# Evicting the P-times-V bank in two halves, by VectorE and by a pinned ScalarE copy

## The chip, the cores and the metric

The kernel runs on one core of a Trainium2 chip. The metric is device time in microseconds of one execution, the median over several; a profile of one execution stands beside it. The engines are called PE (TensorE matmul), PEld (TensorE weight load), DVE (VectorE), ACT (ScalarE), POOL (GpSimd) and SP (SyncE, which starts transfers).

## The reference

A block with two branches over x of 2048 rows and 640 columns, mixed by a gate per row. Branch a is attention with 32 heads of 20 columns in 4 segments of 512 rows, plus a memory of the segments before; branch b is a gated feed-forward layer of 1728 columns. In float32:

```python
for s in range(4):                                   # segments of 512 rows
    logits = einsum("bhqd,bhkd->bhqk", qs, ks) * scale + causal_mask
    a_dot = einsum("bhqk,bhkd->bhqd", softmax(logits), vs)
    pq = phi(qs)                                     # t + 1 where t > 0, else exp(t)
    a_mem = einsum(pq, M) / (einsum(pq, z) + 1e-6)
    o = g * a_mem + (1 - g) * a_dot                  # g = sigmoid(beta) per head
    M, z = M + phi(ks)^T vs, z + sum(phi(ks))
a = o @ wo
b = (silu(x @ w1) * (x @ w3)) @ w2
return sigmoid((x * gate_w).sum(-1)) * a + (1 - ...) * b
```

## The kernel before

All weights and activations are split into a high and a low part (fp32r), and each projection is three passes over five blocks of 128 input columns: 15 matmuls of 512 columns into one PSUM bank. PE's queue is in the order in which the program is written (`manual_schedule` for PE alone). The other engines' queues are ordered by the framework's scheduler, from a simulated timeline. `here` (L102, `keep_in_program_order`) pins one instruction behind the one that was traced just before it on the same engine; unpinned instructions may pass each other.

The eight PSUM banks are handed out by `bank_tile` (L111) in turn from a list. A bank that a projection holds while it is being filled goes back to the end of the list when it is full (`filled`, L122).

Attention works on quads of four heads, 32 quads in all, one for every 40 slots of the outer loop. The work of a quad `m` is placed in two visits inside the stream of projections, a big one at slot 5 and a small one at slot 17 (`VISITS`, L758). A big visit begins when no projection holds a bank. It issues, on PE, in this order:

- s0 of quad m: queries by keys, to find the row maxima (`s_fill`, L594; DVE reduces each region, L609, "junk")
- t0 and t1 of quad m-1: keys by queries with the maximum already subtracted (`t_fill`, L625; ACT takes the exponential into the tile P, L641; POOL masks the diagonal blocks, L645)
- o of quad m-2: P times V for four heads into one bank (`pv_quad`, L650)
- t3 of quad m-1, s2 of quad m, t2 of quad m-1, s1 of quad m

Each s and t fill takes two banks, o takes one. The big visits of quads 0 and 1 lack o, and that of quad 1 is cut in two; the last two big visits have no s. After the visit the stream of projections goes on: g and u (up, L253; ACT's tanh L514, DVE's products L515 and L521, ACT's rounding of the high part L106), f (down, L555; DVE adds, L563), q and k (L253; ACT rounds L280, exponentials L283 and L284; DVE L285 and L287), v (L381), op (output projection, L805), nd (memory read).

The instruction in question is L659: DVE copies o's bank (128 partitions by 512 columns) to the tile `oq`, and SP stores that to memory (L661).

Of the kernel before, what the change touches and what calls it, by code (L numbers as in the profile page):

```python
# [11 lines left out]
AF = mybir.ActivationFunctionType  # L12
# [5 lines left out]
P = 128  # L18
# [6 lines left out]
SCALE = DH ** -0.5  # L25
BIG = -1.0e38
# [12 lines left out]
def gated_mix(ctx: ExitStack, tc: tile.TileContext, xT, wqk, wv, w13, w2, w2h, wo, beta, out):  # L39
    nc = tc.nc  # L40
# [61 lines left out]
    here = tc.keep_in_program_order  # L102
    last = {}
# [7 lines left out]
    def bank_tile(name, hold=None):  # L111


        k = free.pop(0)
        ps = pp.tile([P, L], F32, tag=f"b{k}", name=name, bufs=1)
        if hold:
            held[k] = -hold
        else:
            free.append(k)
        return ps  # L120
# [348 lines left out]
    def job_q(cs, mb, alloc={}):  # L469
        i = w_add(wqk[mb], D)  # L470
        return [(3.5, q_block(c, mb, i, alloc.get(c))) for c in cs]

    def job_q2(cs, mb, alloc={}):

        i = w_add(wqk[mb], D)
        j = w_add(wqk[mb + 1], D)
        return [(3.5, q_block(c, m, k, alloc.get(c), j if c == cs[-1] and m > mb else i))
                for c in cs for m, k in ((mb, i), (mb + 1, j))]
# [89 lines left out]
    oall, heads, pairs = {}, {}, {}  # L568

    def load_pair(p):  # L570

        j = 2 * p
        c, h = divmod(j, H)
        t = qk[p // 2 % 2][:, :, p % 2]
        for mb in {DH * h // P, (DH * h + 2 * DH - 1) // P}:
            assert ("q", c, mb) in stored and ("k", c, mb) in stored
        assert ("v", c, 3) in stored
        for i in range(2):
            here(nc.gpsimd.dma_start(t[64 * i:64 * i + RH], qkd[c][RH * (h + i):RH * (h + i + 1)]))  # L579
        if h % 8 == 0:  # L580
            bank["v"] = v = vg[j // 8 % NVG]
            here(nc.sync.dma_start(v[:, :, :VG], vd[c][:, :, VE * h:VE * h + VG]))
        if p % 2 == 0:
            bank["m"] = sp.tile([P, 16], F32, tag="m", name=f"m{j}", bufs=2)
        for i in range(2):
            o = VE * (h % 8 + i)
            heads[j + i] = dict(c=c, h=h + i, v=bank["v"][:, :, o:o + 32])
        pairs[p] = dict(t=t, m=bank["m"])
# [5 lines left out]
    def s_fill(m, f):  # L594

        todo = S_FILL[f]
        ps = [bank_tile(f"s{m}_{f}_{i}") for i in range(2)]
        for n, (k, qb, o) in enumerate(todo):
            w = P * (qb + 1)
            for i in range(2):  # L600
                q, key = (pairs[2 * m + k]["t"][64 * i:64 * i + RH, x] for x in range(2))
                nc.tensor.matmul(ps[i][:, o:o + w], q[:, qb * P:(qb + 1) * P], key[:, :w],  # L602
                                 start=n == 0, stop=n == len(todo) - 1, skip_group_check=True)
        for i in range(2):
            for k, qb, o in todo:
                w = P * (qb + 1)
                junk = sp.tile([P, L], BF, tag="junk", name="junk", bufs=1)
                a = 8 * i + 4 * k + qb
                nc.vector.tensor_tensor_reduce(out=junk[:, :w], in0=ps[i][:, o:o + w], in1=mask[:, L - w:],  # L609
                                               scale=1.0, scalar=-3.0e38, op0=ALU.add, op1=ALU.max,  # L610
                                               accum_out=pairs[2 * m]["m"][:, a:a + 1])
# [10 lines left out]
            dst = qk[p // 2 % 2][RH + a:RH + a + 65:64, 0].rearrange("h k (b n) -> h (k b) n", n=P).bitcast(F32)  # L622
            after(4, lambda d=dst, r=16 * a: here(nc.scalar.dma_start(d, mr[r:r + 16])))

    def t_fill(m, f):  # L625

        todo = T_FILL[f]
        ps = [bank_tile(f"t{m}_{f}_{i}") for i in range(2)]
        for n, (k, kb, o) in enumerate(todo):
            u = pairs[2 * m + k]  # L630
            if "P" not in u:
                u["P"] = sp.tile([P, 2, 1280], F32, tag="P32", name=f"P{2 * m + k}", bufs=NP)
            for i in range(2):
                q, key = (u["t"][64 * i:64 * i + RH + 2, w] for w in range(2))
                nc.tensor.matmul(ps[i][:, o:o + L - kb * P], key[:, kb * P:(kb + 1) * P], q[:, kb * P:],  # L635
                                 start=n == 0, stop=n == len(todo) - 1, skip_group_check=True)

        outs = [(k, PSEG[kb][0], o, L if (kb, len(todo)) == (1, 2) else L - kb * P) for k, kb, o in todo if kb != 3]
        for i in range(2):
            for k, o, b, n in outs:  # L640
                last["exp"] = nc.scalar.activation(pairs[2 * m + k]["P"][:, i, o:o + n], ps[i][:, b:b + n],  # L641
                                                   AF.Exp, scale=SCALE)
        for k, o, n in (((0, 0, 1),), ((0, 512, 1),), ((0, 896, 2),), ((1, 0, 1),), ((1, 512, 1), (1, 896, 2)))[f]:
            d = pairs[2 * m + k]["P"][:, :, o:o + n * P].rearrange("p h (a b) -> p h a b", b=P)
            nc.gpsimd.affine_select(d, d, pattern=[[0, 2], [0, n], [1, P]], base=0, channel_multiplier=-1,  # L645
                                    compare_op=ALU.is_ge, fill=0.0)
# [3 lines left out]
    def pv_quad(p):  # L650

        ps = bank_tile(f"o{p}")
        for kb, (o, n) in enumerate(PSEG):
            for i in range(4):
                nc.tensor.matmul(ps[32 * i:32 * i + 32, kb * P:], heads[2 * p + i]["v"][:, kb],  # L655
                                 pairs[p + i // 2]["P"][:, i % 2, o:o + n],
                                 start=kb == 0, stop=kb == 3, skip_group_check=True)
        ot = sp.tile([P, L], F32, tag="oq", name=f"oq{p}", bufs=1)
        nc.vector.tensor_copy(ot, ps)  # L659
        c, h = heads[2 * p]["c"], heads[2 * p]["h"]  # L660
        nc.sync.dma_start(od[c][h:h + 4].rearrange("h e n -> (h e) n"), ot)  # L661
        q = p // 2 % 8
        for b in OUT.get(q, ()):
            after(8, o_load, c, b)
        if q == 7:
            after(6 if c < NSEG - 1 else 2, o_sums, c)
# [77 lines left out]
    def after(n, f, *a):  # L744
        soon.append([n, f, a])

    def tick():
        for e in list(soon):
            e[0] -= 1
            if e[0] <= 0:  # L750
                soon.remove(e)
                e[1](*e[2])
# [4 lines left out]
    BIG, SMALL = 5, 17  # L757
# [3 lines left out]
    def attention():  # L761

        for m in range(-1, NQUAD + 2):
            for n in range(40):
                if m == -1 and n < 40 - LEAD:
                    continue

                todo = VISITS.get(n, ()) if m != 1 else {BIG: VISITS[BIG][:3], BIG + 6: VISITS[BIG][4:]}.get(n, VISITS.get(n, ()))
                todo = [(kind, m - q, f) for kind, q, *f in todo if 0 <= m - q < NQUAD]
                if todo:  # L770
                    yield "amid" if len(todo) < 4 else "between"
                    for kind, q, f in todo:
                        if kind == "o":
                            pv_quad(2 * q)
                        else:
                            (s_fill if kind == "s" else t_fill)(q, *f)
                    if n == SMALL and 0 <= m < NQUAD:
                        after(4, max_rows, 2 * m)
                elif n in ((24, 36) if m < 0 else (BIG + 7, SMALL + 1)) and m + 1 < NQUAD:
                    load_pair(2 * (m + 1) + (n > BIG + 7 if m >= 0 else n > 24))  # L780
                tick()
                yield m
# [118 lines left out]
    q = job_q(B[:1], 0, {2: big_tile})  # L901
# [5 lines left out]
    q = job_q2(B, 3)  # L907
# [21 lines left out]
    for n, (_, g) in enumerate(head):  # L929
# [7 lines left out]
        elif n == 7:  # L937
            gates()
    stores(True)
    att = attention()  # L940

    def begin():
# [102 lines left out]
```

## Time and profile before

| what | value |
|---|---|
| median of 3 runs | 1108.1 us (1107.41 to 1110.36) |
| the profiled execution | 1108.07 us |
| its span, first to last instruction | 1106.4 us |
| PE busy | 1095.1 us, 99% |
| DVE busy | 593.5 us, 54% |
| ACT busy | 381.2 us, 34% |
| POOL busy | 583.3 us, 53% |
| granted TensorE clock | 1.00 |

In the profile's rows, "out<-in" names the tile written and the tiles read; "xcount" is how many instructions a row merges; a time in brackets is how long the engine had been idle and which instruction released it. Matmuls are pipelined and their ends are modelled, so two matmuls' durations overlap, and PE's busy share is no measure of how well it is used. In the timeline the columns are the start and the length of the stretch in us.

### The profile page before, as it was taken

What the parts mean: (1) busy time and instruction counts of PE and PEld (TensorE: products, weight loads), DVE (VectorE), ACT (ScalarE), POOL (GpSimd) and SP (SyncE); (2) the same over time, 40 slices, a digit from 0 to 9 for tenths busy, and PEclk for the clock granted to TensorE, in tenths of its full rate; (3) what the DMA queues carried; (4) which work ended last, traced back from release to release, by engine and by line L of the source; (5) the groups of instructions that cost most, each with busy time, mean ns of one, the idle gap of its engine ahead of it and who ended that gap; (6) DMA issues with size and microseconds to landing.
All of it is one profiled execution on the core that took longest, in us unless ns stands there. A gap on an engine that the chain in (4) does not pass through costs nothing.

```text
span 1106.4 us, 17867 instructions
## 1 busy us (share of the span) xinstructions
PE 1095.1 (99%) x6285; PEld 854.0 (77%) x6285; DVE 593.5 (54%) x1708; ACT 381.2 (34%) x826; POOL 583.3 (53%) x729
## 2 busy tenths in 40 slices
PE   9999999999999999999999999999999999999997
PEld 7988877777777777787977777777777777777786
DVE  5032564355555554366154678875557665551645
ACT  6244233343233122145244543424333332233120
POOL 5055556366366363565175547556764555565253
PEclk9999999999999999999999999999999999999999
DMA  8266943335165132535268967455654443432122
GB/s 314 102 212 220 281 117 82 95 82 127 47 164 125 57 78 94 156 98 191 96 202 271 287 204 193 103 157 138 166 139 111 103 104 90 117 105 86 52 79 95
DMA packets 87545, 153.20 MB, mean 138 GB/s; under 512 B 11584, under 2 KB 25184, under 8 KB 87456
## 3 DMA queue, kind: packets, MB, share of 16 engines
q1 hardware_dynamic: 63040, 106.30, 30.5%
q0 software_dynamic: 20384, 38.68, 15.6%
q10 hardware_dynamic: 4032, 7.08, 1.8%
q8 instruction: 50, 0.82, 0.3%
q14 instruction: 39, 0.32, 0.1%
HBM read 96.56 MB, written 54.54 MB: 137 GB/s over the span
## 4 chain that ended last, share of the span: by engine, by line
PE 94%; DVE 3%; ACT 1%; DMA 1%; issue 1%; ACTq 0%; SPq 0%; DVEq 0%
PE g L253 17%; PE u L253 16%; PE f L555 16%; PE k L253 6%; PE v L381 6%; PE op L805 6%; PE o L655 6%; PE q L253 5%; PE s L602 5%; PE t L635 4%; PE nd L348 1%; PE pm L445 1%; PE q L323 1%; DVE junk L609 1%; PE pkt L430 1%
## 5 line engine op out<-in xcount | busy, mean ns | idle before, releaser
L609 DVE CUSTOM_DVE_ANT_0 junk<-s,mask 128x256 bf16<-128x256 f32 (+3 forms) x512 | 250.3, 489 | 105.9 <-PE s L602 73.6
L641 ACT ACTIVATE P<-t 128x512 f32<-128x512 f32 (+1 forms) x384 | 172.4, 538 | 190.5 <-PE t L635 153.3
L253 PE MATMUL g<-X,W 128*128 128x512 f32 x840 | 208.7, 398 | 0.0
L175 POOL TENSOR_TENSOR W<-wr,W 128x640 fp32r<-128x640 f32 (+1 forms) x126 | 200.2, 1595 | 2.3
L174 POOL CAST W<-wr 128x640 fp32r<-128x640 f32 (+1 forms) x126 | 90.9, 726 | 208.9 <-PE f L555 47.0
L253 PE MATMUL u<-X,W 128*128 128x512 f32 x780 | 196.8, 399 | 0.0
L555 PE MATMUL f<-ht,W 128*128 128x512 f32 x820 | 196.6, 397 | 0.0
L645 POOL TENSOR_SCALAR_AFFINE_SELECT P<-P 128x256 f32<-128x256 f32 x192 | 94.0, 498 | 181.1 <-ACT P L641 180.7
L253 PEld LDWEIGHTS g<-X,W 128*128 128x128 f32 x840 | 156.0, 188 | 36.5 <-issue 0.4
L555 PEld LDWEIGHTS f<-ht,W 128*128 128x128 f32 x820 | 152.8, 188 | 36.5 <-DVE acc L536 0.4
L253 PEld LDWEIGHTS u<-X,W 128*128 128x128 f32 x780 | 144.1, 188 | 34.4 <-ACT P L641 0.3
L107 POOL TENSOR_TENSOR ht<-ft,ht 128x512 fp32r<-128x512 f32 x52 | 67.0, 1289 | 91.9 <-ACT ht L106 91.3
L579 POOL DMA_DIRECT2D qk<-qkd x128 | 83.3, 652 | 0.3
L602 PE MATMUL s<-qk 60*128 60x256 f32 (+3 forms) x512 | 78.2, 346 | 1.3 <-DVE fu L515 1.0
L253 PE MATMUL k<-X,W 128*128 128x512 f32 x300 | 77.0, 404 | 0.0
L655 PE MATMUL o<-P,vg 128*32 128x512 f32 (+3 forms) x1024 | 75.5, 436 | 1.4 <-DVE on L735 1.4
L514 ACT ACTIVATE ft<-g 128x512 f32<-128x512 f32 x52 | 31.1, 599 | 125.8 <-PE g L253 114.8
L381 PE MATMUL v<-W,X 128*128 128x320 f32 (+1 forms) x480 | 71.9, 311 | 0.4 <-ACT P L641 0.4
L515 DVE SCALAR_TENSOR_TENSOR fu<-ft,g 128x512 f32<-128x512 f32 x52 | 35.6, 685 | 68.3 <-ACT ft L514 59.2
L381 PEld LDWEIGHTS v<-W,X 128*128 128x128 f32 x480 | 71.0, 189 | 1.1 <-ACT P L641 0.6
L106 ACT CAST ht<-ft 128x512 fp32r<-128x512 f32 x52 | 32.2, 619 | 112.0 <-DVE ft L521 111.9
L563 DVE TENSOR_TENSOR acc<-f,acc 128x512 f32<-128x512 f32 x65 | 44.7, 689 | 44.8 <-PE f L555 44.6
(120 smaller groups left out, 1200.6 us busy)
## 6 DMA issues: line engine op xcount, KB each, us to landing
qk<-qkd POOLq DMA_DIRECT2D x128, 240.0 KB, 4.2
wr<-in_w_dram SPq DMA_DIRECT2D x80, 320.0 KB
qkd<-qs SPq DMA_DIRECT2D x20, 512.0 KB
qkd<-ks SPq DMA_DIRECT2D x20, 512.0 KB
od<-oq SPq DMA_DIRECT2D x32, 256.0 KB
wr<-in_wo_dram SPq DMA_DIRECT2D x20, 320.0 KB
vg<-vd SPq DMA_DIRECT2D x16, 336.0 KB
xr<-in_xT_dram SPq DMA_DIRECT2D x20, 256.0 KB
```

The costliest lines, as they stand in the source:

```text
L107: (lo or nc.gpsimd.tensor_sub)(dst[:, 1], src, dst[:, 0].bitcast(F32))
L174: nc.gpsimd.tensor_copy(w[:, 0, :n], raw[:, :n])
L175: nc.gpsimd.tensor_sub(w[:, 1, :n], raw[:, :n], w[:, 0, :n].bitcast(F32))
L253: nc.tensor.matmul(ps, w[:, a, kb * P:(kb + 1) * P], x[:, b, kb, :], start=n == 0, stop=n == 14)
L381: nc.tensor.matmul(ps[:, :n1 - n0], x[:, a, kb, lb * P:(lb + 1) * P], wvt[kb][:, b, n0:n1], start=n == 0, stop=n == 14)
L555: nc.tensor.matmul(ps, w, h, start=n == 0, stop=n == len(ms) - 1)
L579: here(nc.gpsimd.dma_start(t[64 * i:64 * i + RH], qkd[c][RH * (h + i):RH * (h + i + 1)]))
L602: nc.tensor.matmul(ps[i][:, o:o + w], q[:, qb * P:(qb + 1) * P], key[:, :w], start=n == 0, stop=n == len(todo) - 1, skip_group_check=True)
L609: nc.vector.tensor_tensor_reduce(out=junk[:, :w], in0=ps[i][:, o:o + w], in1=mask[:, L - w:], scale=1.0, scalar=-3.0e38, op0=ALU.add, op1= ...
L641: last["exp"] = nc.scalar.activation(pairs[2 * m + k]["P"][:, i, o:o + n], ps[i][:, b:b + n], AF.Exp, scale=SCALE)
L645: nc.gpsimd.affine_select(d, d, pattern=[[0, 2], [0, n], [1, P]], base=0, channel_multiplier=-1, compare_op=ALU.is_ge, fill=0.0)
L655: nc.tensor.matmul(ps[32 * i:32 * i + 32, kb * P:], heads[2 * p + i]["v"][:, kb], pairs[p + i // 2]["P"][:, i % 2, o:o + n], start=kb == 0 ...
```

## The change

`pv_quad` copies the first 256 columns of o's bank on DVE and the other 256 on ACT. ACT's copy is pinned by `here`, so it stands behind the ACT instruction traced before it, the last exponential of t1. `t_fill` takes a `pin`, and in the big visits all its exponentials are pinned in the same way: those of t3 and t2 stand behind the copy, and the first of t0 stands behind whatever ACT instruction was traced ahead of the visit. The small visits and the second part of quad 1's cut visit are not pinned.

```diff
-    def t_fill(m, f):
+    def t_fill(m, f, pin=lambda ins: ins):
...
         for i in range(2):
             for k, o, b, n in outs:
-                last["exp"] = nc.scalar.activation(pairs[2 * m + k]["P"][:, i, o:o + n], ps[i][:, b:b + n],
-                                                   AF.Exp, scale=SCALE)
+                last["exp"] = pin(nc.scalar.activation(pairs[2 * m + k]["P"][:, i, o:o + n], ps[i][:, b:b + n],
+                                                       AF.Exp, scale=SCALE))
...
         ot = sp.tile([P, L], F32, tag="oq", name=f"oq{p}", bufs=1)
-        nc.vector.tensor_copy(ot, ps)
+        nc.vector.tensor_copy(ot[:, :256], ps[:, :256])
+        here(nc.scalar.copy(ot[:, 256:], ps[:, 256:]))
...
                         if kind == "o":
                             pv_quad(2 * q)
+                        elif kind == "s":
+                            s_fill(q, *f)
                         else:
-                            (s_fill if kind == "s" else t_fill)(q, *f)
+                            t_fill(q, *f, *([here] if n == BIG and q == m - 1 else []))
```

## The prediction

> **What bounds the kernel now.** I read the totals of the page first, then the tile of the eviction, then the timeline of single visits, engine by engine, and last the chain of waits in the same windows.
>
> ```profile
> span 1106.4 us, 17867 instructions
> PE 1095.1 (99%) x6285; PEld 854.0 (77%) x6285; DVE 593.5 (54%) x1708; ACT 381.2 (34%) x826; POOL 583.3 (53%) x729
> PE 94%; DVE 3%; ACT 1%; DMA 1%; issue 1%; ACTq 0%; SPq 0%; DVEq 0%
> L659 DVE COPY oq<-o x32: 676/692/692, 174.7 to 1024.3; 128x512 f32<-128x512 f32 x32
> ```
>
> TensorE sets the end: 94% of the chain is PE, and DVE and ACT are idle for half the span and more. Taking 0.27 us of work from DVE 32 times therefore saves nothing by itself. What counts is whether PE stands still in the visit in which the eviction lies. The profiled execution took 1108.07 us, 1.7 us more than its span; the median of the three runs is 1108.1 us, so I add to 1108.07.
>
> A full visit fills banks in the order s0, t0, t1, o, t3, s2, t2, s1, and it starts with all eight free. Counting banks off the list: s0 takes the first and second, t0 the next two, t1 the next two, o the seventh, t3 the eighth and, again, the first; s2, t2 and s1 go round as far as the seventh. So the second half of s1 gets o's bank, and the projection behind the visit gets the eighth, which the first exponential of t3 has to leave. Here is a typical visit after o: PE, DVE and ACT from the timelines, the last line from the chain in that window.
>
> ```profile
> 469.41 0.50 PE L635 MATMUL t<-qk 62*128 62x512 f32 x2
> 469.54 0.69 DVE L659 COPY oq<-o 128x512 f32<-128x512 f32 x1 [1.09 <-PE o L655]
> 470.00 0.60 ACT L641 ACTIVATE P<-t 128x512 f32<-128x512 f32 x1 [0.96 <-PE t L635]
> 470.21 0.58 PE L602 MATMUL s<-qk 60*128 60x384 f32 x4
> 470.72 0.50 PE L555 MATMUL f<-ht,W 128*128 128x512 f32 x1
> 470.37 0.42 PE s L602 x3
> ```
>
> The copy ends at 469.54+0.69 = 470.23. The four matmuls of s1 take 0.58 us. In a visit where o's bank was free in time they take 0.40 us:
>
> ```profile
> 560.99 0.60 ACT L641 ACTIVATE P<-t 128x512 f32<-128x512 f32 x1 [0.46 <-PE t L635]
> 561.22 0.40 PE L602 MATMUL s<-qk 60*128 60x384 f32 x4
> 561.64 0.19 PEld L253 LDWEIGHTS k<-X,W 128*128 128x128 f32 x1 [0.23 <-ACT P L641]
> 561.38 0.23 PE s L602 x4
> ```
>
> The chain, the last line of each fence, says the same (0.42 against 0.23). So the copy costs PE 0.58-0.40 = 0.18 us a visit. The same rows show the second gate. At 561 the projection waits for ACT: the exponential of t3 ends at 560.99+0.60 = 561.59 and PE goes on at 561.64, 0.05 later. In the typical visit that exponential ends at 470.60, so the projection could not start before 470.65 however early o's bank came free. Of the 0.18 us at most 470.72-470.65 = 0.07 can be had.
>
> **What the change costs, part by part.** *The two halves.* Neither a DVE nor an ACT copy of 256 columns stands in the trace; the nearest rows are these.
>
> ```profile
> L609 DVE CUSTOM_DVE_ANT_0 junk<-s,mask 128x512 bf16<-128x512 f32 x128 | 88.2, 689 | 50.2 <-PE s L602 42.7
> L609 DVE CUSTOM_DVE_ANT_0 junk<-s,mask 128x256 bf16<-128x256 f32 x128 | 54.3, 424 | 38.1 <-PE s L602 30.9
> L389 ACT COPY V<-v 128x320 f32<-128x320 f32 x24 | 10.3, 427 | 35.7 <-PE v L381 35.7
> L449 ACT COPY mt<-pm 128x147 f32<-128x147 f32 x12 | 3.4, 284 | 16.8 <-PE pm L445 14.8 <-POOL W L175 2.0
> ```
>
> The 512-wide junk (689 ns) costs what the 512-wide copy does (692), so DVE's half takes the 256-wide 0.42 us. ACT's copies rise by (427-284)/(320-147) = 0.83 ns a column, which gives 0.37 us for 256.
>
> *Do the halves run side by side?* This is the question that decides the sign. Both read one bank. The trace has one place where ACT and DVE read the same bank without one needing the other's result: L283 (ACT) and L285 (DVE) both read the bank of a q or k projection; L285 also needs L280, not L283.
>
> ```profile
> 63.72 0.59 ACT L280 CAST ks<-k 128x512 fp32r<-128x512 f32 x1 [1.14 <-PE k L253]
> 64.20 0.61 ACT L283 ACTIVATE phi_t<-k 128x512 f32<-128x512 f32 x1
> 64.84 0.69 DVE L285 TENSOR_TENSOR ks<-k,ks 128x512 fp32r<-128x512 f32 x1 [2.23 <-ACT phi_t L283]
> 583.47 0.58 ACT L280 CAST ks<-k 128x512 fp32r<-128x512 f32 x1 [1.75 <-DMA wr<-in_wqk_dram]
> 584.09 0.69 DVE L285 TENSOR_TENSOR ks<-k,ks 128x512 fp32r<-128x512 f32 x1 [1.64 <-ACT ks L280]
>   DVE ks L285: 38.5, 12
>   DVE qs L285: 21.4, 10
> ```
>
> Without L283 (the last segment's keys, 583) DVE starts 0.04 us after L280 has ended. With it (63) an idle DVE sits through all of L283 and starts at 64.84, 0.03 after L283's end at 64.81 and 0.53 after L280's at 64.31. The last two rows, from what waited for L283, count 22 such waits among 30 executions. So the build lets two engines read one bank only in turn, in program order. Those readers cover the same columns and the halves do not; that disjoint columns would be let through is the case left open. The Trainium skill ("PSUM — Partial Sum Buffer", section "PSUM bank collisions raise a hardware error") closes it: two engines may not touch the same bank and quadrant at once, reads against reads included, on disjoint columns too. By that rule the halves go in turn and the sum is the +5.6 us below; without it, the first rival's -2.0 us stays possible.
>
> *The visit, redone with halves in turn.* DVE's half runs from 469.54 to 469.96. ACT's half then starts 0.03 later (the latency of 64.81 to 64.84), at 469.99: the moment at which the exponential of t3 now starts (470.00). It ends at 470.36. From there two branches:
> - o's bank comes free at 470.36 instead of 470.23, so the second half of s1 and all behind it move by 0.13 us.
> - The six exponentials of t3 and t2 are traced behind the copy and are pinned to it one by one. How long the copy holds ACT follows from the rows of the exponentials, which overlap:
>
> ```profile
> 466.97 2.06 ACT L641 ACTIVATE P<-t 128x512 f32<-128x512 f32 x4 [18.16 <-PE t L635]
> 470.00 2.19 ACT L641 ACTIVATE P<-t 128x512 f32<-128x512 f32 x6 [0.96 <-PE t L635]
> L641 ACT ACTIVATE P<-t 128x256 f32<-128x256 f32 x128 | 39.1, 413 | 0.0
> ```
>
> Four 512-wide ones in 2.06 us with a last one of 0.60 make (2.06-0.60)/3 = 0.49 us from start to start. Two 512-wide and four 256-wide in 2.19 make (2.19-2x0.49-0.41)/3 = 0.27 us for 256 columns. So the first exponential of t3 starts at 469.99+0.27 = 470.26 instead of 470.00, ends at 470.86, and the projection starts at 470.91 instead of 470.72: **0.19 to 0.20 us later**. The first branch alone would put it at 470.85; the exponential is last. The full latency of the copy in place of 0.27 would make 0.30 us the upper end; the lower is the 0.13 us of the first branch.
>
> *The pins on t0 and t1.* The first exponential of a visit is pinned behind whatever ACT instruction was traced before it. Behind a u projection that is the CAST of L106, which the trace has after the first exponential:
>
> ```profile
> 678.69 0.69 DVE L521 SCALAR_TENSOR_TENSOR ft<-fu,u 128x512 f32<-128x512 f32 x1
> 678.97 0.60 ACT L641 ACTIVATE P<-t 128x512 f32<-128x512 f32 x1 [3.53 <-PE t L635]
> 679.47 0.61 ACT L106 CAST ht<-ft 128x512 fp32r<-128x512 f32 x1
> 679.97 1.57 ACT L641 ACTIVATE P<-t 128x512 f32<-128x512 f32 x3
> 681.53 0.69 DVE L659 COPY oq<-o 128x512 f32<-128x512 f32 x1 [0.70 <-PE o L655]
> ```
>
> The CAST must wait for L521 (678.69+0.69+0.03 = 679.41); four exponentials follow from 679.91 and ACT is free at 679.91+4x0.49 = 681.87. ACT's half could not start before 681.53+0.42+0.03 = 681.98. This late case still has 0.11 us to spare, so the pins on t0 and t1 cost nothing here; they would cost their whole excess beyond that. Behind g, down and output projections the order of the trace is already the pinned one.
>
> *What else moves.* PE's s1 now waits for ACT instead of DVE; nothing else in PE's queue is touched. The store of oq (SP) starts 0.13 us later; its readers come many microseconds later. GpSimd's masks of t3 and t2 follow their exponentials 0.27 us later and are read by the next visit but one's o. DVE's 0.27 us fall into time in which it waits for PE.
>
> **The sum.** 32 copies. The last two visits have no s1 behind the copy: 0. Two visits (the one at 557 and one of its kind behind a q projection) already have t3 delayed by DVE's L287, and there the pin brings L284 forward and gives about as much as the copy takes: 0. That leaves 28 x 0.20 = **+5.6 us**, so 1113.7 us. By the bounds it is 28 x 0.13 = 3.6 to 28 x 0.30 = 8.4 us: 1111.7 to 1116.5.
>
> **Rivals.** *The halves overlap after all (0.10), the other side.* If readers of disjoint columns are let through, ACT's half ends at 469.54+0.37 = 469.91 and holds ACT until 469.81, ahead of the exponential at 470.00. The wait of s1 is gone, the exponential is untouched, and the projection starts at 470.65: 28 x 0.07 = 2.0 us faster, 1106.1. It decides if ACT's half starts within 0.1 us of DVE's. Against it stand the 22 waits of L285.
>
> *The pins reach the copy late (0.08).* Visits behind a u projection, or with an output projection's normalisation traced just ahead, may find ACT busy past 469.99 of their own clock. With eight such visits at 0.3 us more each it is 2.4 us on top: 1116.1. For it: 0.11 us of slack in the late case above. Against: the other visits have their L521 earlier.
>
> *The loss is absorbed (0.05).* If the projections behind the visits were to wait anyway, for weights or for a bank, the end would not move: 1108.1. Against it is the chain: it runs through PE without a break into those projections.
>
> **How the numbers follow.** The first case, halves in turn, gets 0.77. The predicted time is its 1113.7 us; its own range is 1111.7 to 1116.5. The remaining 0.10+0.08+0.05 are the rivals. The range is 1108.0 to 1117.5: it takes in the first case, the absorbed one and most of the late pins, and leaves out the overlap. A change under 0.3% (3.3 us) cannot be told from none with three runs of before between 1107.41 and 1110.36. The first case is slower by more than that but for its lowest end (0.72 of 0.77), late pins are (0.08): 0.80 slower. Same is that low end, absorption and most of the overlap, whose 2.0 us are inside the bound: 0.16. Faster is 0.04, the overlap if the exponentials also come sooner.
>
> **What would show it.** In the changed profile: DVE's oq copy near 0.42 us and ACT's near 0.37, ACT's starting 0.03 after DVE's end; the first exponential of t3 0.27 us after ACT's copy; the projection behind a visit 4.70 us after the visit's first matmul (470.72-466.21 = 4.51 before, by the first row below); PE waiting there for ACT L641. Copies that start together, or a projection at or under 4.51 us, would make the prediction wrong; so would exponentials of t0 that begin more than 1.5 us into the visit.
>
> ```profile
> 466.21 0.51 PE L602 MATMUL s<-qk 60*128 60x512 f32 x2
> ```

## The result and the profile after

The changed kernel takes 1113.81 us in the median (1113.36 to 1113.93) against 1108.65 us before, four executions of each: a recorded ratio of 1.0038, 95% interval 1.0025 to 1.0052 (the quotient of the two medians is 1.0047). The change makes the kernel some 5 us slower; by the interval it is 3 to 6 us. The profiled execution has a span of 1112.1 us, 5.7 us more than before. Here are the totals of the page, then the rows of the tile `oq` (durations min/median/max in ns), then one row of what ACT waited for (total us, times, longest):

```profile
span 1112.1 us, 17915 instructions
PE 1100.5 (99%) x6285; PEld 854.1 (77%) x6285; DVE 584.8 (53%) x1708; ACT 389.8 (35%) x858; POOL 582.7 (52%) x729
```

```profile
L659 DVE COPY oq<-o x32: 423/424/425, 175.7 to 1030.1; 128x256 f32<-128x256 f32 x32
L660 ACT COPY oq<-o x32: 372/372/374, 176.1 to 1030.6; 128x256 f32<-128x256 f32 x32
```

```profile
ACT oq L660 <- DVE oq L659: 24.6, 27, 3.6
```

DVE's work fell by 8.7 us and ACT's rose by 8.6, as the split intends, and PE's busy time, which includes its stalls inside a visit, rose by 5.4. The last row is the finding: ACT's half waited for DVE's half, 27 times of 32. In the other five ACT had hardly been idle or not at all; in all 32 its half starts 0.03 to 0.08 us after DVE's has ended. The same visit as before the change, from the timelines of PE, DVE, ACT and PEld:

```profile
469.37 0.53 PE L602 MATMUL s<-qk 60*128 60x512 f32 x2
472.73 0.42 DVE L659 COPY oq<-o 128x256 f32<-128x256 f32 x1 [1.11 <-PE o L655]
473.19 0.37 ACT L660 COPY oq<-o 128x256 f32<-128x256 f32 x1 [0.95 <-DVE oq L659]
473.46 0.60 ACT L641 ACTIVATE P<-t 128x512 f32<-128x512 f32 x1
473.40 0.71 PE L602 MATMUL s<-qk 60*128 60x384 f32 x4
474.11 0.30 PEld L555 LDWEIGHTS f<-ht,W 128*128 128x128 f32 x2 [0.21 <-ACT P L641]
```

DVE's half ends at 473.15, ACT's starts at 473.19, and the exponential of t3 0.27 us after that, at 473.46. It ends at 474.06 and the projection starts at 474.11, released by ACT. The s1 matmuls take 0.71 us (0.58 before, 0.40 without a wait). From its first matmul to the projection the visit lasts 474.11-469.37 = 4.74 us; before it was 4.51.

Measured in the same way over the 30 big visits that have an s fill behind the copy: 25 are longer by 0.20 to 0.23 us, which makes 5.2 us; the five others differ by -0.05, +0.01, +0.01, +0.09 and +0.43, together 0.5. Two small visits, each behind a big one that a memory read follows, are 0.21 us shorter and give 0.4 back. Stretches between visits shift by up to 1 us in both directions and sum to +0.3. Together that is the 5.7 us of the span.

### The profile page after: what moved, and what is told of

Its sections match the earlier page's. It is cut to its first block, busy times and chain, and to the rows that moved or that the text cites. A ratio compares the mean times of both kernels' runs of the same rounds, so it can differ in the third digit from the quotient of the medians.

```text
span 1112.1 us, 17915 instructions
## 1 busy us (share of the span) xinstructions
PE 1100.5 (99%) x6285; PEld 854.1 (77%) x6285; DVE 584.8 (53%) x1708; ACT 389.8 (35%) x858; POOL 582.7 (52%) x729
## 4 chain that ended last, share of the span: by engine, by line
PE 93%; DVE 3%; ACT 1%; DMA 1%; issue 1%; ACTq 0%; POOL 0%; SPq 0%; DVEq 0%; POOLq 0%
PE g L253 17%; PE f L555 16%; PE u L253 16%; PE op L808 6%; PE k L253 6%; PE v L381 6%; PE o L655 6%; PE s L602 5%; PE q L253 5%; PE t L635 4%; PE nd L348 2%; PE pm L445 1%; PE q L323 1%; DVE junk L609 1%; PE pkt L430 1%
## 5 line engine op out<-in xcount | busy, mean ns | idle before, releaser
L641 ACT ACTIVATE P<-t 128x512 f32<-128x512 f32 (+1 forms) x384 | 171.1, 542 | 136.9 <-PE t L635 100.0
L555 PE MATMUL f<-ht,W 128*128 128x512 f32 x820 | 196.4, 396 | 0.0
L555 PEld LDWEIGHTS f<-ht,W 128*128 128x128 f32 x820 | 152.7, 188 | 37.0 <-ACT P L641 1.4
L602 PE MATMUL s<-qk 60*128 60x256 f32 (+3 forms) x512 | 82.1, 351 | 1.3 <-DVE fu L515 1.0
L515 DVE SCALAR_TENSOR_TENSOR fu<-ft,g 128x512 f32<-128x512 f32 x52 | 35.6, 685 | 71.3 <-ACT ft L514 61.1
L602 PEld LDWEIGHTS s<-qk 60*128 60x128 f32 x512 | 47.0, 185 | 28.7 <-issue 20.3
```

What stands on the lines that cost most here:

```text
L555: nc.tensor.matmul(ps, w, h, start=n == 0, stop=n == len(ms) - 1)
L641: last["exp"] = pin(nc.scalar.activation(pairs[2 * m + k]["P"][:, i, o:o + n], ps[i][:, b:b + n], AF.Exp, scale=SCALE))
```

## Experiments

The theory: two readers of one PSUM bank go in turn, so ACT's half starts where the exponential of t3 used to start, and that exponential releases the next projection 0.2 us later. The rivals: the pins on t0 and t1 cost the time; the late release of o's bank is all of it; ACT's copy costs whatever bank it reads. A last one, that the halves queue for the tile `oq`, which both write, and not for the bank, is taken up further down.

**The pins alone.**

```diff
-        nc.vector.tensor_copy(ot[:, :256], ps[:, :256])
-        here(nc.scalar.copy(ot[:, 256:], ps[:, 256:]))
+        nc.vector.tensor_copy(ot, ps)
```

> DVE copies all 512 columns of o's bank as before; all exponentials of the big visits stay pinned as in the change. Theory in turn (the halves wait for each other on one bank, and ACT's copy pushes the exponential of t3): the pins alone leave the visit at 4.51 us, +0.0 to +0.5 us against before, near 1108.7. Rival pins (the loss comes from exponentials of t0 that wait behind the CAST of the feed-forward layer): about as slow as the change, 1113 to 1114.

Measured: 1108.58 us, ratio to before 0.9997 (0.9987 to 1.0007). The pins cost nothing that can be seen. ACT's timeline behind a u projection shows why: the CAST now comes first, four exponentials follow in 2.06 us, and ACT still idles for 0.38 us ahead of t3.

```profile
342.77 0.62 ACT L106 CAST ht<-ft 128x512 fp32r<-128x512 f32 x1 [3.53 <-DVE ft L521]
343.30 2.06 ACT L641 ACTIVATE P<-t 128x512 f32<-128x512 f32 x4
345.73 0.60 ACT L641 ACTIVATE P<-t 128x512 f32<-128x512 f32 x1 [0.38 <-PE t L635]
```

**No pins at all, with the halves.**

```diff
-        here(nc.scalar.copy(ot[:, 256:], ps[:, 256:]))
+        nc.scalar.copy(ot[:, 256:], ps[:, 256:])
...
-                            t_fill(q, *f, *([here] if n == BIG and q == m - 1 else []))
+                            t_fill(q, *f)
```

> Both halves as in the change, with no pin on the copy nor on any exponential. In ACT's queue the first exponential of t3 then stands ahead of the copy. Theory in turn: ACT's half starts at 3.79+0.48 = 4.27 us of the visit and ends at 4.64, s1's second half starts at 4.70 instead of 4.08, and the projection 0.62 us later than before: in 27 visits +17 us, 1125. Rival pins (the pins are what costs): faster than the change, 1109 or less.

Measured: 1125.08 us, ratio 1.0155 (1.0142 to 1.0168). Without its pin the copy falls behind the first exponential of t3, and s1 waits for it on PE:

```profile
478.05 0.42 DVE L659 COPY oq<-o 128x256 f32<-128x256 f32 x1 [1.09 <-PE o L655]
478.50 0.60 ACT L641 ACTIVATE P<-t 128x512 f32<-128x512 f32 x1 [0.95 <-PE t L635]
479.00 0.37 ACT L660 COPY oq<-o 128x256 f32<-128x256 f32 x1
479.42 0.50 PE L602 MATMUL s<-qk 60*128 60x384 f32 x3 [0.37 <-ACT oq L660]
```

So the pins do what they are for: given halves in turn, they are worth 11 us by the medians.

**ACT's half first.**

```diff
-        nc.vector.tensor_copy(ot[:, :256], ps[:, :256])
         here(nc.scalar.copy(ot[:, 256:], ps[:, 256:]))
+        nc.vector.tensor_copy(ot[:, :256], ps[:, :256])
```

> Both halves as in the change, but ACT's is written first and DVE's second. ACT's half then runs at 3.33 to 3.70 us of the visit and is out of the way when t3 is ready (3.70), DVE's from 3.74 to 4.16. Theory in turn: s1's second half starts at 4.22 as in the change, the exponential of t3 starts at 3.79 as before; the projection starts at 4.64 (4.71 in the change, 4.51 before): 0.13 us in 27 visits, +3.6 us, 1112. If the late release of the bank were all of the loss, the time would stay that of the change (1113.8); if the exponential were all of it, that of before (1108.6); if the halves overlapped in this order, 1107.

Measured: 1112.71 us, ratio 1.0042 (1.0028 to 1.0057). The visit shows that the two branches are apart (ACT, DVE, then PE):

```profile
471.09 0.37 ACT L659 COPY oq<-o 128x256 f32<-128x256 f32 x1 [0.50 <-PE o L655]
471.49 0.42 DVE L660 COPY oq<-o 128x256 f32<-128x256 f32 x1 [1.49 <-ACT oq L659]
471.55 2.19 ACT L641 ACTIVATE P<-t 128x512 f32<-128x512 f32 x6
467.76 0.50 PE L602 MATMUL s<-qk 60*128 60x512 f32 x2
471.76 0.71 PE L602 MATMUL s<-qk 60*128 60x384 f32 x4
472.40 2.36 PE L555 MATMUL f<-ht,W 128*128 128x512 f32 x9
```

Now DVE's half waits for ACT's, in all 32 visits (46.5 us in all). The exponential of t3 is back at 471.55-467.76 = 3.79 us of the visit, s1 still takes 0.71 us, and the projection starts at 4.64: 0.13 us for the bank, and in the change another 0.07 to 0.10 for the exponential. By whole times the order of the halves cannot be told apart: the two intervals overlap, and only the visits carry this verdict.

**ACT's half left out.**

```diff
+    oq = cp.tile([P, L], F32, name="oq")
...
+        nc.gpsimd.memset(oq, 1.0)
...
-        ot = sp.tile([P, L], F32, tag="oq", name=f"oq{p}", bufs=1)
+        ot = oq
         nc.vector.tensor_copy(ot[:, :256], ps[:, :256])
-        here(nc.scalar.copy(ot[:, 256:], ps[:, 256:]))
```

> Leaves out ACT's half: DVE copies 256 columns of o's bank, the other 256 columns of the stored tile hold a constant (so this part of the attention output is not computed). Pins stay. It shows what could be had if o's bank came free early. Theory in turn with two gates: the wait of s1 goes, the exponential of t3 stays where it was (3.79 us into the visit, end 4.39) and releases the projection at 4.44 instead of 4.51: 0.06 us in some 27 visits, 1.7 us faster than before, 1107. Rival one gate (only the bank of o holds PE): 0.17 us a visit, 4.6 us faster, 1104.

Measured: 1107.08 us, ratio 0.9987 (0.9976 to 0.9997). The wait for o's bank is gone (s1 takes 0.40 us) and the visit ends at 470.30-465.83 = 4.47, held by the second gate: the last row, of PEld, waits for the exponential (the edit adds two lines further up, so L602, L641 and L555 are L604, L643 and L557 here).

```profile
465.83 0.53 PE L604 MATMUL s<-qk 60*128 60x512 f32 x2
469.87 0.40 PE L604 MATMUL s<-qk 60*128 60x384 f32 x4
470.30 2.36 PE L557 MATMUL f<-ht,W 128*128 128x512 f32 x9
470.30 0.30 PEld L557 LDWEIGHTS f<-ht,W 128*128 128x128 f32 x2 [0.24 <-ACT P L643]
```

Most visits got 0.06 to 0.08 us shorter. So freeing the bank early brings about 1.6 us here, not the 0.18 us a visit (5 us) of the wait that it removes.

**The whole copy on ACT.**

```diff
-        nc.vector.tensor_copy(ot[:, :256], ps[:, :256])
-        here(nc.scalar.copy(ot[:, 256:], ps[:, 256:]))
+        here(nc.scalar.copy(ot, ps))
```

> ACT copies all 512 columns, pinned; DVE copies none. Theory in turn with two gates: ACT's copy (0.59 us by the 512-wide ACT copies) runs from 3.33 to 3.92 us of the visit, so s1 does not wait; it holds ACT for 0.52 us until 3.85, so the exponential of t3 starts 0.06 later, ends at 4.45 and releases the projection at 4.50, as late as before (4.51): 1108.6, no change. If one copy on ACT delayed the exponentials by more than its hold, up to +5 us.

Measured: 1108.69 us, ratio 1.0001 (0.9992 to 1.0009), no change. ACT needs 588 ns for the whole bank (min/median/max in the row), less than the two halves in turn (424+372 plus the handover). So neither ACT's load nor a longer copy in front of the exponentials is what made the change slow.

```profile
L659 ACT COPY oq<-o x32: 586/588/610, 176.6 to 1025.7; 128x512 f32<-128x512 f32 x32
```

**A bank for each half.** P times V is written to two banks by columns, the first 256 columns first, over the same number of streamed columns:

```diff
-        ps = bank_tile(f"o{p}")
-        for kb, (o, n) in enumerate(PSEG):
-            for i in range(4):
...
+        ps = [bank_tile(f"o{p}_{x}") for x in range(2)]
+        for x in range(2):
+            for kb, (o, n) in enumerate(PSEG[:2 + 2 * x]):
+                a, z = max(kb * P, 256 * x), 256 * x + 256
+                for i in range(4):
+                    nc.tensor.matmul(ps[x][32 * i:32 * i + 32, a:z], heads[2 * p + i]["v"][:, kb],
+                                     pairs[p + i // 2]["P"][:, i % 2, o + a - kb * P:o + z - kb * P],
+                                     start=kb == 0, stop=kb == 1 + 2 * x, skip_group_check=True)
...
-        nc.vector.tensor_copy(ot[:, :256], ps[:, :256])
-        here(nc.scalar.copy(ot[:, 256:], ps[:, 256:]))
+        nc.vector.tensor_copy(ot[:, :256], ps[0][:, :256])
+        here(nc.scalar.copy(ot[:, 256:], ps[1][:, 256:]))
```

> The change with its cause taken away: DVE's half, ACT's half and all pins as in the change, but each half lies in a bank of its own (columns 0 to 255 first, then 256 to 511; eight more matmuls a visit over the same columns). Theory in turn (one bank is why the halves queue): ACT's half starts when P times V ends, at 3.33 instead of 3.79, holds ACT until 3.60, and the exponential of t3 stays at 3.79: projection at 4.44, 1.7 us faster than before and 7 faster than the change, 1107. Rival (ACT's copy costs by being in ACT's queue ahead of the exponentials, whatever the bank): ACT's half still near 3.79 or the exponential still at 4.06, near 1113.

Measured: 1115.78 us, ratio 1.0062 (1.0049 to 1.0075): the time missed the expectation, and the visits say where. Behind f, u and op the theory holds: ACT's half starts when P times V ends, and the projection comes at 473.17-468.72 = 4.45 us.

```profile
468.72 0.50 PE L602 MATMUL s<-qk 60*128 60x512 f32 x2
472.06 0.37 ACT L662 COPY oq<-o 128x256 f32<-128x256 f32 x1 [0.50 <-PE o L657]
473.17 2.36 PE L555 MATMUL f<-ht,W 128*128 128x512 f32 x9
```

Behind a g projection PE stops in the middle of P times V, for the DVE instruction that still reads g's bank; first a row of PEld's timeline, then who waited, over the whole run, for that instruction, L515, and for L287, which reads the banks of q and k (total us, times):

```profile
248.48 1.45 PEld L657 LDWEIGHTS o<-P,vg 128*32 128x32 f32 x32 [0.39 <-DVE fu L515]
```

```profile
  PEld o L657: 3.2, 8
  PEld o L657: 4.4, 3
```

The second half of P times V takes the eighth bank of the visit, and that is the one that the projection left last. The eight visits behind g got 0.28 us longer, and the three behind q and k 1.0 to 1.5 us. The variant in which DVE copies both halves and nothing is pinned did the same:

> No ACT copy and no pins. P times V is written to two banks by columns, 0 to 255 first (keys blocks 0 and 1), then 256 to 511, with eight more matmuls a visit over the same number of columns; DVE copies each half from its bank. The first half is copied while PE still fills the second. Theory: the second half leaves at 3.33+0.42 = 3.75, s1 does not wait, and the exponential of t3 (4.39) releases the projection at 4.44: 0.06 us in 27 visits, 1.7 us faster than before, 1107. If the narrower matmuls cost PE time, slower by that: 0.1 us a visit would make +1 us.

Measured: 1116.56 us, ratio 1.0075 (1.0062 to 1.0088), with 0.27 to 0.28 us behind g and 1.8 to 3.3 us behind q and k.

**Past the bank just left.** The second half takes the bank after the next one:

```diff
-    def bank_tile(name, hold=None):
+    def bank_tile(name, hold=None, skip=0):
...
-        k = free.pop(0)
+        k = free.pop(skip)
...
-        ps = [bank_tile(f"o{p}_{x}") for x in range(2)]
+        ps = [bank_tile(f"o{p}_{x}", skip=x if p < 2 * (NQUAD - 2) else 0) for x in range(2)]
```

> The kernel with own banks for the halves (DVE's and ACT's half, pins), but the second half of P times V takes the bank after the next one, so that it does not land in the bank that the projection before the visit has just left. Theory: the 0.28 us that e7_own_banks lost in each visit behind a g projection, and its 1.0 to 1.5 us in those behind q and k, came from the wait for that bank; they go, every full visit gets the 0.06 us that e7_own_banks gained behind f, u and op, and the time is 1106.5 to 1107.5 (before 1108.5). Rival (the eight narrower matmuls or their banks cost by themselves): still slower than before, 1109 or more.

Measured: 1107.41 us, ratio 0.9986 (0.9977 to 0.9994). By the medians this version beats the kernel before by 1.5 us and the change by 6.4 us. It has the halves, the engines and the pins of the change; the banks differ and, with them, the order of P times V:

```profile
465.95 0.50 PE L602 MATMUL s<-qk 60*128 60x512 f32 x2
469.29 0.37 ACT L662 COPY oq<-o 128x256 f32<-128x256 f32 x1 [0.51 <-PE o L657]
470.39 2.36 PE L555 MATMUL f<-ht,W 128*128 128x512 f32 x9
```

The visit is 4.44 us long, behind g as behind f.

One thing changes together with the banks. As the first columns are filled first, DVE's half ends 0.06 to 1.51 us before ACT's starts, and the two copies never meet. The times alone therefore leave open whether the halves of the change queue for the bank or for the tile `oq`, which both write. The semaphores (the counters by which an engine tells another that it is done) in the traces decide it: in the change ACT's copy waits for DVE's semaphore in all 32 visits; with a bank for each half, in both versions, it waits for PE's in all 32 and for DVE's in none, although both halves still write `oq`. And the kernel before already has two engines writing different columns of one tile at the same time: GpSimd's mask of t0 (the first row, columns 0 to 127 of a tile P) runs during the exponentials of t1 (the last two of the second row, columns from 512 on):

```profile
468.13 0.42 POOL L645 TENSOR_SCALAR_AFFINE_SELECT P<-P 128x256 f32<-128x256 f32 x1 [7.33 <-ACT P L641]
466.97 2.06 ACT L641 ACTIVATE P<-t 128x512 f32<-128x512 f32 x4 [18.16 <-PE t L635]
```

Last, the banks of this version without ACT:

> The same banks, with DVE copying both halves and no pins. By the theory the visit is as long as with ACT's half (the projection is released by the exponential of t3 in both): 1106.5 to 1107.5, except behind k and q, where t3 waits for DVE's L287 as before. If taking work from DVE was worth something by itself, e8_skip_bank is faster than this one by more than 1 us.

Measured: 1108.25 us, ratio 0.9992 (0.9984 to 1.0001), 0.75 us above the expected range, and not to be told from the kernel before. In the common visits it is as short as the other one. It loses 0.13 to 0.20 us in the three visits behind q and k, where the other gains 0.09 to 0.26: without pins exponentials pass L284 on ACT, the copy of the first half stands ahead of L287 on DVE, and t3 waits for L287. The two intervals overlap, so that difference is read from the visits alone. The other version is 0.84 us faster, less than the 1 us named above: that taking work from DVE is worth something by itself is not shown.

What was not tried: both engines reading one bank at the same moment, without the order between them.

## Why the prediction was right

**The bound and the two gates.** Right. s1's wait for o's bank and the projection's wait for the exponential of t3 were read as 0.18 and 0.07 us; with the first taken away (the half left out) most visits shortened by 0.06 to 0.08 us. One reading was off and nothing hangs on it: DVE is idle for 46% of the span, not for half and more.

**The durations.** The estimates 0.42 and 0.37 us were measured as 424 and 372 ns. Taking DVE's from a reduction of the same width and ACT's from the slope between two copies was good to 1%.

**The halves in turn.** This decided the sign. The 22 waits of L285 were evidence for equal columns only. The 27 waits of L660 show it for disjoint columns. Own banks removed them: ACT's half then starts when P times V ends instead of 0.46 us later, and waits for no semaphore of DVE's. The rule of the Trainium skill ("PSUM — Partial Sum Buffer", section "PSUM bank collisions raise a hardware error") agrees with what this build does; that the hardware itself would go wrong without the order no run here shows.

**Which branch is last.** Predicted: the exponential, at 0.20 us, ahead of the bank, at 0.13. Measured: 0.21, with PE waiting for ACT L641 in the rows of after, and 0.13 with ACT's half first.

**The pins.** Predicted at no cost; the kernel with the pins alone shows it.

**The count.** The prediction took 28 visits at 0.20 and two at 0. It was 25 at about 0.21, and the other five have reasons of their own. The two taken at 0, where the pin brings L284 forward, came out at -0.05 and +0.01; the pins alone gain 0.19 and 0.13 us there. The visit at 511 was expected to lose like the rest and lost 0.01: its t fills wait for DVE's additions of an f projection (L563), which ended 0.84 us into the visit instead of 1.10, so P times V started 0.27 us earlier. Why DVE was earlier there is open. One at 699 lost 0.09; there, too, the pins alone gain 0.13. The one at 949 lost 0.43, but half of that, 0.21 us, lies in its s fill, ahead of the copy, at a wait that varies between executions (below). Two losses were given back in the small visits, which the sum had left out: behind a memory read the next small visit had been waiting already, 0.4 us for DVE's L354. These errors nearly cancel. The base moved as well: the sum was added to 1108.07, and the median before came out at 1108.65, so the change by the medians is 5.2 us and not 5.6. That 1113.7 lies so close to 1113.81 is therefore partly luck; 0.2 us a visit is what the prediction got right.

**The absorbed loss**, a rival at 0.05, thus happened in two visits of thirty.

## What to carry to other kernels

Splitting the eviction of one PSUM bank between two engines is no split in this build: the halves go in turn, and the fixed part of each copy is paid twice (0.42+0.04+0.37 us in place of 0.69). Give each half a bank of its own, and check which instruction still reads the bank it takes over. Before shortening a wait, look for the next gate behind it: here a wait of 0.18 us could give back 0.07 at most.

## What the runs showed of the hardware that was not expected

The eight additional matmuls a visit, with 128 or 256 columns instead of up to 512, cost PE nothing that can be seen: P times V takes 2.36 us in the 32 matmuls of the rows and 2.37 in 48 (each matmul of the program stands there twice), by the first two rows below, from PE's timelines (ACT's half first, and the version past the bank just left). One visit, 949 us into the run, varies between executions of like kernels: its s fill waits up to 1.5 us for a transfer to land (the third row, from the waits of the kernel with pins alone), and this one visit moved by +0.1 to +3.1 us across the profiles. A difference of 1 us in span is therefore not read from one profile here.

```profile
468.66 2.36 PE L655 MATMUL o<-P,vg 128*32 128x512 f32 x32
```

```profile
466.85 2.37 PE L657 MATMUL o<-P,vg 128*32 128x256 f32 x48
```

```profile
PE s L602 <- DMA qk<-qkd: 1.5, 1, 1.5
```
